# Query projection in unpadded 128-column tiles, laid into head slots through DRAM, with the VectorE exponential pairs placed anew

## The chip, the cores and the metric

The kernel runs on one core of a Trainium2 chip. The metric is device microseconds of one execution. Before the change the median of three runs is 865.13 us (864.38 to 865.44).

TensorE (PE) multiplies, ScalarE (ACT) evaluates exponentials, VectorE (DVE) and GpSimd (POOL) do elementwise work, and SyncE (SP) issues nearly all DMAs. Each engine works through its own list in order. Only semaphores tie the lists together.

## The reference

Two branches share the input x = A_q (2048 tokens by 640 features, bf16) and are mixed by a gate per token:

```python
g = _sigmoid((x * gate_w).sum(-1, keepdims=True))
a = _A_ref(x, A_k, A_v, A_shift_k, A_ssm_k, A_ssm_D)   # q * (long convolution of shifted k * v)
b = _B_ref(x, B_wq, B_wk, B_wv, B_wo)
return g * a + (1 - g) * b
```

Branch b is attention with 32 query heads of 20 features and one shared key and value head:

```python
q = (x @ wq).reshape(B, S, H, Dh)      # H = 32, Dh = 20, so wq is 640 x 640
k = x @ wk                             # 2048 x 20
v = x @ wv
scores = einsum("bhqd,bkd->bhqk", q, k) * (Dh ** -0.5)
o = einsum("bhqk,bkd->bhqd", softmax(scores), v)
return o.reshape(B, S, H * Dh) @ wo
```

Attention needs 32 x 2048 x 2048 exponentials. Branch a is a causal convolution along the tokens for each feature, done as a discrete Fourier transform by matrix products.

## The kernel before

**Attention tiles.** The 2048 queries are taken in four blocks I of 512. Within a block the 32 heads form 8 groups of 4. A group number G = 8 I + g runs from 0 to 31. For each group and each of 16 key chunks j, four 32-row matmuls (`score`, L1243) make four score tiles of 128 keys by 512 queries, one for each head slot r. So there are 32 x 16 x 4 = 2048 tiles. A head slot is 32 partitions: rows 32 r to 32 r + 19 of `qT` hold the 20 features of head 4 g + r, row 32 r + 20 holds an estimate of that query's norm (it makes a shift that keeps the exponential in range), and row 32 r + 21 holds a constant. `qT0` serves even blocks and `qT1` odd ones.

**Who does the exponential.** `stream` (L1197) strings the tiles together and cuts what is ACT's into units of three and two tiles by turns. L1280 is ACT's exponential of one unit, out of PSUM into `ETA` (three tiles) or `ETB` (two). The table `DVE_J` (L666) names, for each group, the key chunks of which two of the four tiles go to DVE instead. Such a pair costs DVE two PSUM reads (L1313, `dW`) and three passes over 128 x 1024 (L1325 and L1326, `dX`; L1328, `ETd`). `DVE_J` holds 108 pairs: 22, 31, 24 and 31 in the four blocks. L1333 multiplies the exponentials with the values into PSUM bank 6. At a group's end L1407 copies that bank to `acc`; then `norm` goes by four small DMAs on SP and one POOL product (L1419).

**The query projection.** `qproj` (L1140) works on padded weights: `wq_pad` has 1024 columns, 32 for each head, of which 20 are filled. POOL clears it (five memsets, L1032) and copies the weights in from `wqst` (L1024, and four copies at L1036). A group then takes five matmuls 128 x 512 (L1148), one DVE move out of PSUM that adds the constant row (L1159; ACT's L1161 for the first), and one square (L1163). For each batch of groups, matmuls with an indicator matrix (L1171) sum the squares by head, DVE takes an approximate root by integer arithmetic (L1177, `cr`), and one DMA (`crow`) puts the norms into rows 20, 52, 84 and 116. Block 0 is done in batches of 1, 2, 2, 2 and 1 groups, later blocks in two batches of four (`qproj_next`, L1737). Its PSUM banks are 7 and 5, which it shares with DVE's score tiles and with the convolution.

**The order of the work.** `Scheduler` (L172) plays the whole program through at build time. It has a cost for every operation (`c_dve`, `c_pool`, `c_act` and literals in the calls), a latency between engines (`LATS` before attention starts, `LATM` and `LATX` after), and priorities. It places each operation when its engine is free and its inputs are there, and it knows a port that DVE and POOL share (`port=True`, L508 to L513). The order that comes out is fixed in each engine's list. The two main streams of attention (scores, exponentials) keep their own order; everything else is fitted between. Matmuls on zeros (L1772) are put where PE would be idle.

**The convolution** (`kshift`, `conv`, `spectra`, `mac`, `inverse`) and the output projection fill PE, DVE and POOL between attention's pieces. The last block's part of the output is made by `part` and `tail`.

Of the kernel before, what the change touches and what calls it, by code (L numbers as in the profile page):

```python
# [5 lines left out]
dt = mybir.dt  # L6
# [18 lines left out]
        ("pool", "pool"): 0.0}  # L25
# [146 lines left out]
class Scheduler:  # L172
# [148 lines left out]
    def lat_of(self, op, a, b):  # L321
        if self.main_started:
            return LATM.get((a, b), LATX)
        return 0.03 if op.kind == "d" else LATS.get((a, b), LAT)
# [341 lines left out]
DVE_J = ((), (2,), (4, 6, 10, 14), (2, 6, 13, 14), (1, 2, 4, 11), (7, 12, 14), (3, 10), (2, 9, 11, 12), (1, 4, 7, 10, 12, 14), (1, 9), (1, 4, 8, 10, 14), (2, 7, 12), (2, 7, 8, 13), (2, 5, 9, 13), (6, 10, 13), (1, 3, 11, 13), (), (2, 11, 14), (1, 2, 4, 9), (1, 7, 9, 13), (2, 4, 6, 10, 14), (1, 7, 10, 14), (), (2, 7, 11, 14), (5, 6, 12, 14), (3, 7, 9, 12), (3, 6, 9, 10, 12), (13,), (2, 5, 6, 14), (4, 5, 8), (1, 4, 6, 9, 11, 14), (1, 2, 4, 5))  # L666
# [35 lines left out]
class Kernel:  # L702
# [59 lines left out]
    def alloc(self):  # L762
# [23 lines left out]
        sb("wq_pad", [128, NDC, 1024], BF16)  # L786
# [21 lines left out]
        sb("IndG4", [128, 4, 16], BF16)  # L808
# [14 lines left out]
        sb("cr", [16, 512], BF16)  # L823
# [22 lines left out]
        over("wqst", "qT1", 0, [128, NDC, D], BF16)  # L846
# [12 lines left out]
        over("wog", "wq_pad", 0, [128, 8, D], BF16)  # L859
# [6 lines left out]
        self.ps_bf = self.ps[:, :].bitcast(BF16)  # L866
        self.scr_o = nc.dram_tensor("scr_o", [4, 1024, 512], BF16).ap()
# [3 lines left out]
    def loads(self):  # L871
# [3 lines left out]
        for b in range(NB):  # L875
# [4 lines left out]
            if b == 0:  # L880
                self.dma(T["wqst"][:, :, 0:80], wq[:, :, 0:80], writes=[("wqst", 0)], prio=-8.5, lat=5.0)
# [6 lines left out]
        self.dma(T["wqst"][:, :, 80:640], wq[:, :, 80:640], writes=[("wqst", 1)], nbytes=716800, prio=-4,  # L888
# [5 lines left out]
    def consts(self):  # L894
# [28 lines left out]
        for n in ("IndG2", "IndG4"):  # L923
            P(lambda e, n=n: e.memset(T[n][:, :, :], 0.0), (), [n], 0.2, prio=-9.7)
# [34 lines left out]
    def tables2(self):  # L959
# [7 lines left out]
        for gl in range(4):  # L967
            self.dve(lambda e, gl=gl: e.tensor_copy(T["IndG4"][:, gl, gl:16:4], T["acol"][:, :]), ["acol"], ["IndG4"],
                     0.15, **k)

# [19 lines left out]
        for name, parts in (("Tsin", (("Tsin", 1), ("Tcos", 1), ("Tsin", -1), ("Tcos", -1))),  # L990
                            ("Tcos", (("Tcos", 1), ("Tsin", -1), ("Tcos", -1), ("Tsin", 1)))):
            for r, (src, sg) in enumerate(parts):
                for c in range(H):
# [5 lines left out]
                    self.pool(fn, [(src, c)], [(name, H + c, r), (name, H + c)], c_pool(256), prio=15.0 + c,  # L999
# [13 lines left out]
    def weights(self):  # L1013
# [9 lines left out]
        src = T["wqst"][:, :, :].rearrange("p k (h c) -> p k h c", c=20)  # L1023
# [3 lines left out]
    def weights2(self):  # L1027
        T = self.T
        dst = T["wq_pad"][:, :, :].rearrange("p k (h c) -> p k h c", c=32)
        src = T["wqst"][:, :, :].rearrange("p k (h c) -> p k h c", c=20)  # L1030
        for k in range(NDC):
            self.pool(lambda e, k=k: e.memset(T["wq_pad"][:, k, 128:1024].bitcast(I32), 0), (), [("wq_pad", g) for g in range(1, 8)], 0.45,  # L1032
                      prio=-8.9, after=[self.g.writer["sq", 0]])
        self.wq_cp = []
        for lo, hi in ((4, 8), (8, 16), (16, 24), (24, 32)):
            self.wq_cp.append(self.pool(lambda e, lo=lo, hi=hi: e.tensor_copy(dst[:, :, lo:hi, 0:20], src[:, :, lo:hi, :]),  # L1036
                      [("wqst", 1)], [("wq_pad", g) for g in range(lo // 4, hi // 4)], 0.75 if hi - lo == 4 else 1.5, prio=-4 + 0.01 * lo, name="wq_cp",
                      after=self.crow0 + [self.g.writer["kT4", NB - 1, 0]]))
# [101 lines left out]
    def qproj(self, I, gs, prio, banks, ng):  # L1140

        T = self.T
        qt = T[f"qT{I % 2}"]
        par = I % 2
        for gl, gi in enumerate(gs):
            gr = self.group("qp", prio, banks=banks)
            for dc in range(NDC):
# [4 lines left out]
                if dc == 0:  # L1152

                    o.deps.update(self.crow0 or ())
                    if self.crow0:
                        o.deps.add(self.g.writer["mcol"])
                    o.deps.update(self.g.readers.get((f"qT{par}", gi), ()))
            self.evac(gr, "dve", None, ["qup"], [(f"qT{par}", gi)], 0.7,
# [6 lines left out]
                     [(f"qT{par}", gi)], [("sq", gl)], 0.336 if I else 0.43, prio=-1500.0 if I == 0 and gs[0] < 3 else prio - 500, port=True,  # L1165
# [4 lines left out]
        for gl in range(nq):  # L1170
# [10 lines left out]
                 writes=[(f"qT{par}", gi) for gi in gs], nbytes=4 * nq * 1024, prio=pr, name="crow", lat=1.7)  # L1181
        if I == 0 and gs[0] == 0:
            self.crow0 = [o]

# [33 lines left out]
    def attention(self):  # L1218
# [19 lines left out]

        def score(e, bk, G, j, r, t=0):
# [10 lines left out]
        def QK(n):  # L1250
            un = units[n]
            I = min(un[-1][0], LASTG) // 8
            if I not in started:
                started.add(I)
                self.qproj_next(I)
                if I == NB - 1:
                    self.g.fence(["oT3", "part"], ["xT"])
                    self.g.fence(["wog"], ["wq_pad"])
# [3 lines left out]
            for p, (t, k, (G, j, r)) in enumerate(parts):  # L1262
                bk = base[n % 2] + k
                c = 0.003
                if p == len(parts) - 1 or parts[p + 1][0] > t:
                    c = 0.216 / min(split(x[0]) for u, _, x in parts if u == t)
                o = op("pe", lambda e, bk=bk, G=G, j=j, r=r, t=t: score(e, bk, G, j, r, t),
                       [self.kkey(split(G) * j + t), qkey(G)], [("ps", bk)], c,
# [15 lines left out]
        def DEXP(G, j):  # L1284
# [12 lines left out]
            for h, r in enumerate(self.on_dve[G, j]):  # L1297
# [7 lines left out]
                        [self.kkey(m * j + t) for t in range(m)] + [qkey(G)], 0.04)  # L1305
# [97 lines left out]
    def norm(self, I, g):  # L1403
# [8 lines left out]
        self.dve(lambda e: e.reciprocal(T["rcp"][:, :], T["den"][:, :]), ["den"], ["rcp"], 0.3, prio=p, name="rcp")  # L1412
# [22 lines left out]
    def part(self):  # L1435

        T = self.T
        for ci in range(4):
            for half in range(2):
# [3 lines left out]
                for g in range(6):  # L1443
# [5 lines left out]
                    ALU.mult, ALU.add), ["omgf", ("A", i)], [("part", ci)], c_dve(HD))  # L1449
# [27 lines left out]
    def tail(self):  # L1477
# [11 lines left out]
        for ci in range(fin[0]):  # L1489
            i = 4 * (NB - 1) + ci  # L1490
            osb = T[f"outsb{ci}"]
            for half in range(2):
                n0 = HD * half
                gr = self.group("op2s", -800.0 + ci, banks=(7, 6, 5))
                for g in (6, 7):
# [4 lines left out]
                    ALU.mult, ALU.add), ["omgf", ("part", ci)], [("outsb", ci)], c_dve(HD))  # L1500
# [37 lines left out]
    def kshift(self):  # L1538
# [7 lines left out]
        for b in range(NB):  # L1546
# [10 lines left out]
            ["ident", "wtap"], ["kdiag"], c_ps(2560), prio=16, port=True, name="ksh", after=[self.g.writer["kT4", NB - 1, 0], self.wq_cp[1]])  # L1557
# [24 lines left out]
    def conv(self):  # L1582
        T = self.T
        t0, per = 120.0, 100.0
        for i in range(NSC):

            self.dve(lambda e, i=i: e.tensor_scalar(T["xn"][:, i, :], T["xn"][:, i, :], T["gf"][:, i:i + 1], None,
                                                    ALU.mult), ["gf"], [("xg", i), ("xn", i // 4)], 0.4,
# [9 lines left out]
    def spectra(self, c, fc, base):  # L1598
# [7 lines left out]
        for kind in ("X", "K"):  # L1606
# [26 lines left out]
            if kind == "X":  # L1633
# [11 lines left out]
                [("K", p)], c_dve(256))  # L1645
# [186 lines left out]
```

## Time and profile before

| what | value |
|---|---|
| median of three runs | 865.13 us |
| the profiled execution | 866.22 us |
| its span, first to last instruction | 864.4 us |
| granted TensorE clock, mean | 0.998 |
| first exponential of attention (L1280) starts | 20.46 us |
| last exponential of attention starts | 857.79 us |
| DMA moved | 30.69 MB in 49728 packets |

The profiled execution is 1.1 us above the median, and its span is 1.8 us shorter than its time. Differences are worked out inside the span and set against the median.

A row of a group of instructions reads: line, engine, operation, output<-input with shapes, count | busy us, mean ns of one | idle us of the engine just before them, and what ended it. ACT's and PE's instructions overlap in their pipelines, so for ACT the distance between the ends of successive instructions is the honest cost, not the mean duration. A row of the timeline reads: start us, length us, engine, line, operation, count, and in brackets the idle time before it with its releaser. A row of windows reads: stretch, its length, and for each engine the busy us and the count.

### The profile page before, as it was taken

The page shows a single profiled execution, that of the slowest core. Times are in us where ns is not written, and L with a number is a line of the kernel's source. Part 1 is how long each engine was busy: PE and PEld are TensorE (multiplying, and loading weights), DVE is VectorE, ACT ScalarE, POOL GpSimd, SP SyncE. Part 2 cuts the span into 40 slices and gives each one's busy share as a digit, 9 for nine tenths or more (in the row PEclk, how much of TensorE's full clock was granted, in tenths as well). Part 3 has the DMA queues.
Part 4 walks back from the last instruction along what each step waited for, and adds up shares of the span by engine and source line. Part 5 has one row for each costly group of instructions (what it writes and reads, how often), then busy time and mean ns, then how long its engine had stood idle before and what let it go on. Part 6 is the DMA issues. An engine that isn't in the chain of part 4 may idle for free.

```text
span 864.4 us, 18503 instructions
## 1 busy us (share of the span) xinstructions
PE 840.7 (97%) x7963; PEld 350.2 (41%) x7963; DVE 782.3 (90%) x987; ACT 845.7 (98%) x755; POOL 375.7 (43%) x315
## 2 busy tenths in 40 slices
PE   8999999999999999999999999999999999999998
PEld 5234433344334433434434334444443434433334
DVE  7689999998999899999898989898869999898896
ACT  6999999999999999999999999999999999999997
POOL 4584000458764243655434475335776665000010
PEclk9999999999999999999999999999999999999999
DMA  6900010000100000020000020200010000401111
GB/s 172 236 14 9 20 45 20 16 19 8 44 20 21 20 14 17 13 44 20 20 14 8 20 45 20 53 20 8 26 38 20 15 2 24 102 30 60 43 35 44
DMA packets 49728, 30.69 MB, mean 36 GB/s; under 512 B 32493, under 2 KB 45678, under 8 KB 49646
## 3 DMA queue, kind: packets, MB, share of 16 engines
q1 hardware_dynamic: 49070, 29.29, 12.5%
q8 instruction: 62, 1.02, 0.5%
q10 hardware_dynamic: 576, 0.22, 0.1%
q14 instruction: 20, 0.16, 0.1%
HBM read 17.85 MB, written 6.02 MB: 28 GB/s over the span
## 4 chain that ended last, share of the span: by engine, by line
ACT 45%; PE 27%; DVE 24%; issue 2%; POOL 1%; POOLq 0%; DVEq 0%
ACT ETA L1280 27%; ACT ETB L1280 18%; PE ps L1243 8%; DVE dX L1326 6%; DVE ETd L1328 5%; DVE dX L1325 4%; PE ps L1333 4%; PE ps L1622 4%; DVE dW L1313 4%; PE ps L1690 3%; PE ps L1772 2%; PE ps L1720 2%; DVE qT L1159 1%; DVE X L1635 1%; PE ps L1777 1%
## 5 line engine op out<-in xcount | busy, mean ns | idle before, releaser
L1280 ACT ACTIVATE ETA<-ps 128x1536 bf16<-128x1536 f32 (+1 forms) x367 | 566.6, 1544 | 6.0 <-PE ps L1243 5.3
L1280 ACT ACTIVATE ETB<-ps 128x1024 bf16<-128x1024 f32 x366 | 411.2, 1123 | 0.2 <-PE ps L1243 0.2
L1243 PE MATMUL ps<-qT,kT 32*128 32x512 bf16 (+2 forms) x2176 | 304.1, 372 | 10.4 <-ACT ETA L1280 2.8
L1655 POOL TENSOR_TENSOR Pp<-X,K 128x1024 f32<-128x1024 bf16 (+1 forms) x80 | 150.7, 1896 | 130.1 <-DVE K L1643 62.9
L1243 PEld LDWEIGHTS ps<-qT,kT 32*128 32x128 bf16 x2176 | 78.1, 91 | 234.3 <-ACT ETB L1280 102.4
L1313 DVE TENSOR_SCALAR dW<-ps 128x512 f32<-128x512 f32 x216 | 147.0, 681 | 26.2 <-PE ps L1243 25.7
L1328 DVE SCALAR_TENSOR_TENSOR ETd<-dX,dW 128x1024 int16<-128x1024 f32 x108 | 158.5, 1467 | 3.0 <-PE ps L1333 2.7
L1326 DVE SCALAR_TENSOR_TENSOR dX<-dX,dW 128x1024 f32<-128x1024 f32 x108 | 154.1, 1427 | 0.7
L1333 PE MATMUL ps<-ETA,vaug 128*32 128x512 bf16 (+2 forms) x1174 | 154.1, 372 | 0.1
L1325 DVE SCALAR_TENSOR_TENSOR dX<-dW 128x1024 f32<-128x1024 uint16 x108 | 151.5, 1403 | 1.3
L1333 PE MATMUL ps<-ETB,vaug 128*32 128x512 bf16 (+2 forms) x778 | 148.1, 373 | 0.2 <-ACT ETA L1280 0.2
L1655 POOL TENSOR_TENSOR AB<-Pp 128x256 bf16<-128x256 f32 x80 | 71.7, 896 | 72.7 <-DVE dX L1326 26.6
L1622 PE MATMUL ps<-ssm_kT,Tcs 128*128 128x256 bf16 x600 | 89.8, 274 | 2.5 <-DVE dW L1313 2.0
L1690 PE MATMUL ps<-AB,Tcs 128*128 128x256 bf16 x600 | 89.7, 276 | 0.3 <-DVE dW L1313 0.2
L1622 PE MATMUL ps<-kv,Tcs 128*128 128x256 bf16 x600 | 87.1, 275 | 0.7 <-DVE dW L1313 0.4
L1419 POOL TENSOR_TENSOR oTn<-acc,rbc 128x512 bf16<-128x512 f32 x24 | 38.8, 1616 | 85.6 <-DMA rbc<-scr_d 67.3
L1655 POOL TENSOR_TENSOR Pp<-Pp 128x512 f32<-128x512 f32 x40 | 53.7, 1342 | 42.3 <-DVE dX L1325 12.9
L1622 PEld LDWEIGHTS ps<-ssm_kT,Tcs 128*128 128x128 bf16 x600 | 50.6, 98 | 38.5 <-issue 26.8
L1690 PEld LDWEIGHTS ps<-AB,Tcs 128*128 128x128 bf16 x600 | 51.6, 98 | 34.2 <-issue 25.7
L1622 PEld LDWEIGHTS ps<-kv,Tcs 128*128 128x128 bf16 x600 | 49.8, 98 | 35.1 <-issue 24.0
L1772 PE MATMUL ps<-Tcs,zeros 128*32 128x512 bf16 (+1 forms) x724 | 61.5, 383 | 0.4 <-DVE acc L1407 0.3
L1419 POOL TENSOR_TENSOR oT<-acc,rbc 128x512 bf16<-128x512 f32 x7 | 10.1, 1449 | 108.3 <-DMA rbc<-scr_d 58.1
(136 smaller groups left out, 664.9 us busy)
## 6 DMA issues: line engine op xcount, KB each, us to landing
rbc<-scr_d SPq DMA_DIRECT2D x31, 256.0 KB
scr_o<-oTn SPq DMA_DIRECT2D x24, 128.0 KB, 1.7
kv<-in_A_v_dram SPq DMA_DIRECT2D x4, 640.0 KB, 5.0
out_dram<-outsb SPq DMA_DIRECT2D x15, 160.0 KB, 1.8
xn<-in_A_q_dram SPq DMA_DIRECT2D x3, 640.0 KB, 7.9
oTp<-scr_o SPq DMA_DIRECT2D x12, 160.0 KB, 2.5
wog<-in_B_wo_dram SPq DMA_DIRECT2D x4, 200.0 KB
wo<-in_B_wo_dram SPq DMA_DIRECT2D x4, 200.0 KB
```

The lines of the kernel that those rows point to most:

```text
L1243: return e.matmul(self.bank(bk, n, n * t), T["kT4"][32 * r:32 * r + 32, 128 * jt:128 * jt + 128], T[k][32 * r:32 * r + 32, g, q0:q0 + n], ...
L1280: op("act", lambda e: e.activation(et(n)[:, 0:w], self.ps[:, lo:lo + w], ACT.Exp, scale=SCALE), [("ps", base[n % 2] + k) for k in range(le ...
L1313: self.evac(gr, "dve", lambda e, bk, c=c: e.tensor_scalar(W[:, c], self.bank(bk), SCALE * LOG2E * 128.0, 128.0 * (127 - KDN) - 32768.0, AL ...
L1325: V(lambda e: e.scalar_tensor_tensor(X[:, :], w, DP, w, ALU.add, ALU.mult), [kW], ["dX"], c_dve(1024), **k)
L1326: V(lambda e: e.scalar_tensor_tensor(X[:, :], X[:, :], DQ, w, ALU.add, ALU.mult), [kW], ["dX"], c_dve(1024), **k)
L1328: V(lambda e: e.scalar_tensor_tensor(E, X[:, :], DA, W[:, :], ALU.mult, ALU.add), [kW, "dX"], [("ETd", pe)], c_dve(1024), **k)
L1333: return op("pe", lambda e: e.matmul(self.bank(b, n)[32 * r:32 * r + 32, :], T[va][:, j, :], src, start=(j == 0), stop=(j == NSC - 1), til ...
L1419: self.pool(lambda e: e.tensor_tensor(out, T["acc"][:, :], T["rbc"][:, :], ALU.mult), ["acc", "rbc"], [key], 1.27, prio=p, port=True, name ...
L1622: self.mm(gr, lambda e, bk, lhs=lhs, rhs=rhs, comp=comp, n=n: e.matmul(self.bank(bk, 256, 256 * comp), lhs, rhs, start=(n == 0), stop=(n = ...
L1655: f = lambda e: e.tensor_tensor(out, a, b, alu)
L1690: self.mm(gr, lambda e, bk, lhs=lhs, fc=fc, comp=comp, h=h: e.matmul(self.bank(bk, 256, 256 * h), lhs, AB[:, fc, :, comp, :], start=(fc == ...
L1772: sch.filler, *sch.filler2 = ([[lambda e, r=r, st=st, b=b, n=n: e.matmul(self.bank(b, n)[32 * r:32 * r + 32, :], self.T["zeros"][:, 0:32], ...
```

## The change

The projection drops the padding for all but the first two groups of block 0. A tile is now 128 consecutive columns of the raw `wq`, five tiles for 640 columns, so that a tile holds 6.4 heads that cross the head slots. `qtiles` moves each tile from PSUM to a staging area (in `qT1` for block 0, in the used-up part of `xT` for later blocks), squares it, and stores it to a DRAM tensor `scr_q`. Four DMAs, one for each slot r, then read it back with the 20 features of a head as 20 partitions. One product with a new indicator `IndT` (made by `heads`) gives the norms of all heads of the block at once, and four DMAs put them in place. The constant row and the zero padding no longer come with the projection: `qfixed` writes them beforehand, for `qT0` by one POOL copy and one DMA that repeats it, for `qT1` by eight POOL copies. Groups 0 and 1 of block 0 keep the old way, with `wq_pad` cut to 256 columns, and block 0 starts its tiles at tile 1. A score matmul waits on three records now (features, norms, slot).

Apart from that, costs and latencies in the planner are changed at some ten places, and `DVE_J` is written anew: 110 pairs, with 21, 32, 27 and 30 in the four blocks.

```diff
-        ("pool", "pool"): 0.0}
+        ("pool", "pool"): 0.075}
...
-            return LATM.get((a, b), LATX)
+            return 0.19 if op.name == "dqk" else LATM.get((a, b), LATX)
...
-DVE_J = ((), (2,), (4, 6, 10, 14), (2, 6, 13, 14), (1, 2, 4, 11), (7, 12, 14), (3, 10), (2, 9, 11, 12), (1, 4, 7, 10, 12, 14), (1, 9), (1, 4, 8, 10, 14), (2, 7, 12), (2, 7, 8, 13), (2, 5, 9, 13), (6, 10, 13), (1, 3, 11, 13), (), (2, 11, 14), (1, 2, 4, 9), (1, 7, 9, 13), (2, 4, 6, 10, 14), (1, 7, 10, 14), (), (2, 7, 11, 14), (5, 6, 12, 14), (3, 7, 9, 12), (3, 6, 9, 10, 12), (13,), (2, 5, 6, 14), (4, 5, 8), (1, 4, 6, 9, 11, 14), (1, 2, 4, 5))
+DVE_J = ((), (3,), (4, 6, 11, 14), (3, 8, 14), (1, 2, 5, 10), (7, 12, 13), (3, 11), (2, 9, 10, 12), (1, 4, 7, 11, 12, 14), (1, 12), (2, 4, 8, 10, 14), (2, 7, 11), (1, 6, 9, 13), (5, 8, 13, 14), (6, 8, 13), (1, 3, 10, 13, 14), (12,), (2, 9, 14), (2, 8, 9, 13), (1, 8, 9, 13), (2, 4, 6, 11, 12, 14), (1, 8, 11, 12), (), (1, 8, 11, 13, 14), (2, 6, 10, 13, 14), (7, 14), (1, 3, 6, 9, 12), (6, 11, 14), (4, 7, 12), (1, 7, 10), (1, 4, 6, 8, 10, 12, 14), (3, 5))
...
     def weights2(self):
-        for k in range(NDC):
-            self.pool(lambda e, k=k: e.memset(T["wq_pad"][:, k, 128:1024].bitcast(I32), 0), ...
-        self.wq_cp = []
-        for lo, hi in ((4, 8), (8, 16), (16, 24), (24, 32)):
-            self.wq_cp.append(self.pool(lambda e, lo=lo, hi=hi: e.tensor_copy(dst[:, :, lo:hi, 0:20], src[:, :, lo:hi, :]), ...
+        self.pool(lambda e: e.memset(T["wq_pad"][:, :, 128:256].bitcast(I32), 0), (), [("wq_pad", 1)], 0.5, prio=-8.9,
+                  after=[self.g.writer["sq", 0]])
+        self.wq_cp = self.pool(lambda e: e.tensor_copy(dst[:, :, 4:8, 0:20], src[:, :, 4:8, :]), [("wqst", 1)],
+                               [("wq_pad", 1)], 0.75, prio=-4, name="wq_cp", ...
+    def qfixed(self, I):
+        qt, lo = T[f"qT{I}"], 0 if I else 2
+        f = lambda e, a, b: e.tensor_copy(qt[:, a:b, :], T["qup"][:, 0:1].unsqueeze(2).to_broadcast([128, b - a, 512]))
+        if I:
+            for g in range(8):
+                self.pool(lambda e, g=g: f(e, g, g + 1), ["qup"], [(f"qT{I}", g, x) for x in range(5)], c_pool(512),
+                          prio=40.0 + g, name="qfix", after=self.crow0)
+            return
+        self.pool(lambda e: f(e, 2, 3), ["qup"], [("qT0", 2, x) for x in range(5)], c_pool(512), prio=-5.0,
+                  name="qfix", after=self.crow0)
+        self.dma(qt[:, 3:8, :], qt[:, 2:3, :].to_broadcast([128, 5, 512]), reads=[("qT0", 2, 0)],
+                 writes=[("qT0", g, x) for g in range(3, 8) for x in range(5)], nbytes=655360, prio=0.0, name="qfix")
...
+    def heads(self):
+        self.pool(lambda e: e.iota(u.rearrange("p (t r g) -> p t r g", t=NDC, r=4), [[128, NDC], [-20, 4], [-80, 8]], ...
+        self.dve(lambda e: e.tensor_scalar(v, u, 0.0, None, ALU.is_ge), ["acc"], ["accv"], 0.25, **k)
+        self.dve(lambda e: e.scalar_tensor_tensor(T["IndT"][:, :, :].rearrange("p t c -> p (t c)"), u, 20.0, v, ALU.is_lt, ...
...
+    def qtiles(self, I, t0, prio, banks):
+        for t in range(t0, NDC):
+            gr = self.group("qp", prio, banks=banks)
+            for dc in range(NDC):
+                o = self.mm(gr, lambda e, bk, t=t, dc=dc: e.matmul(
+                    self.bank(bk), T["wq"][:, dc, 128 * t:128 * t + 128], T["xT"][:, dc, 512 * I:512 * I + 512], ...
+            x = self.evac(gr, "dve", None, (), [("qs", I, t)], 0.7,
+                          alts={"dve": ((lambda e, bk, o=stage[t]: e.tensor_copy(o, self.bank(bk))), ...
+            self.dve(lambda e, t=t: e.tensor_tensor(T[f"sq{t}"][:, :], stage[t], stage[t], ALU.mult), [("qs", I, t)],
+                     [("sq", t)], 0.336, prio=prio - 500, port=True, name="sq")
+            self.dma(self.scr_q[I][128 * t:128 * t + 128, :], stage[t], reads=[("qs", I, t)], writes=[("scr_q", I, t)],
+                     nbytes=131072, prio=prio - 500, name="q_st")
+        gr = self.group("q2", prio - 500, banks=banks)
+        for t in range(t0, NDC):
+            self.mm(gr, lambda e, bk, t=t: e.matmul(self.bank(bk)[0:32, :], T["IndT"][:, t, :], T[f"sq{t}"][:, :], ...
...
+        for r in range(4):
+            self.dma(qt[32 * r:32 * r + 20, g0:8, :], src[r][:, g0:8, :], reads=[("scr_q", I, t) for t in range(t0, NDC)],
+                     writes=[(par, g, r) for g in range(g0, 8)], nbytes=163840, prio=prio - 500, name="q_ld", lat=2.6)
+        for r in range(4):
+            self.dma(qt[32 * r + 20:32 * r + 21, g0:8, :], cr[8 * r + g0:8 * r + 8, :], reads=["cr"], ... name="crow", lat=1.7)
...
+        def qks(G, r):
+            n, g = qkey(G)
+            return [(n, g, r), (n, g, 4), (n, g, 5 + r)]
...
     def qproj_next(self, I):
         if I < NB:
-            for b in range(2):
-                self.qproj(I, list(range(4 * b, 4 * b + 4)), 150.0 * (I - 1) + 60 + 60 * b, (7, 5), 4)
+            self.qtiles(I, 0, 150.0 * (I - 1) + 60, (7, 5))
...
-        for b, gs in enumerate(([0], [1, 2], [3, 4], [5, 6], [7])):
-            self.qproj(0, gs, 0.61 if b == 0 else 3.0 + 6 * b, ALLB if b == 0 else (7, 5), 2)
+        self.qproj(0, [0], 0.61, ALLB, 2)
+        self.weights2()
+        self.qproj(0, [1], 9.0, (7, 5), 2)
...
+        self.heads()
+        self.qfixed(0)
+        self.qtiles(0, 1, 12.0, (7, 5))
+        self.qfixed(1)
```

The other planner costs that change are those of the table copies (+0.15), the reciprocal (0.3 to 0.16), the scaled input rows (0.4 to 0.3), the output moves (+0.06), one spectrum move (+0.03), and one POOL product, `mac`'s first, set to 2.125.

## The prediction

> **What bounds the kernel now.** I read the page's shares first, then the chain, then ACT's timeline.
>
> ```profile
> PE 840.7 (97%) x7963; PEld 350.2 (41%) x7963; DVE 782.3 (90%) x987; ACT 845.7 (98%) x755; POOL 375.7 (43%) x315
> ACT 45%; PE 27%; DVE 24%; issue 2%; POOL 1%; POOLq 0%; DVEq 0%
> ```
>
> ACT is busy for 98% of the span and has the largest share of the chain. PE's 97% is not a full load: 724 of its matmuls are products of zeros that the planner puts where PE would be idle. So ACT sets the pace, and the question is what it costs ACT to get through its list. ACT's timeline answers that:
>
> ```profile
> 20.46 1.45 ACT L1280 ACTIVATE ETA<-ps 128x1536 bf16<-128x1536 f32 x1 [0.17 <-PE ps L1243]
> 21.81 1.02 ACT L1280 ACTIVATE ETB<-ps 128x1024 bf16<-128x1024 f32 x1
> 22.71 1.46 ACT L1280 ACTIVATE ETA<-ps 128x1536 bf16<-128x1536 f32 x1
> ...
> 857.79 1.16 ACT L1280 ACTIVATE ETA<-ps 128x1024 bf16<-128x1024 f32 x1
> ```
>
> The first ends at 21.91, the third at 24.17: a unit of three and a unit of two, five tiles, take 2.26 us, or 0.452 us a tile. ACT has 2048 - 2 x 108 = 1832 tiles, so 1832 x 0.452 = 828.1 us without a pause. From 20.46 to 858.95 are 838.5 us, so **10.4 us are stalls**. Before it lie 20.5 us of start, after it 5.5 us of tail. Span = 20.5 + 828.1 + 10.4 + 5.5 = 864.4.
>
> Where do the stalls sit? In stretches of 27 us (columns: PE, PEld, DVE, ACT, POOL busy with counts, clock, DMA):
>
> ```profile
> 108.00:135.00 27.00, 26.03 (x235) 8.49 (x232) 26.85 (x38) 26.59 (x25) 1.57 (x1) 1.00 0.16 36
> 135.00:162.00 27.00, 25.79 (x230) 9.69 (x228) 27.00 (x38) 26.49 (x24) 5.82 (x4) 1.00 0.05 18
> ...
> 648.00:675.00 27.00, 25.41 (x235) 11.14 (x233) 26.79 (x29) 26.18 (x24) 16.59 (x14) 1.00 0.05 16
> ```
>
> ACT loses half a microsecond and more where DVE is full (26.8 to 27.0 of 27). DVE doesn't stand on the path itself; it makes PE wait, and PE is in order. One such place, in the projection:
>
> ```profile
> 119.09 0.74 DVE L1159 TENSOR_SCALAR qT<-ps,cols 128x512 bf16<-128x512 f32 x1
> 119.88 0.39 PE L1148 MATMUL ps<-xT,wq_pad 128*128 128x512 bf16 x1 [0.77 <-DVE qT L1159]
> 120.69 1.45 ACT L1280 ACTIVATE ETA<-ps 128x1536 bf16<-128x1536 f32 x1 [0.41 <-PE ps L1243]
> ```
>
> A projection matmul waits 0.77 us for its bank, the score matmuls queue behind it, and ACT stands for 0.41 us.
>
> **The change, part by part.** *Pairs.* 110 instead of 108 takes 4 tiles from ACT: 4 x 0.452 = **-1.8 us**, the one term that is certain to be on the path. On DVE a pair costs two moves and three passes (sums over 108 pairs; the mean follows the busy time):
>
> ```profile
> L1328 DVE SCALAR_TENSOR_TENSOR ETd<-dX,dW 128x1024 int16<-128x1024 f32 x108 | 158.5, 1467 | 3.0 <-PE ps L1333 2.7
> L1326 DVE SCALAR_TENSOR_TENSOR dX<-dX,dW 128x1024 f32<-128x1024 f32 x108 | 154.1, 1427 | 0.7
> L1325 DVE SCALAR_TENSOR_TENSOR dX<-dW 128x1024 f32<-128x1024 uint16 x108 | 151.5, 1403 | 1.3
> L1313 DVE TENSOR_SCALAR dW<-ps 128x512 f32<-128x512 f32 x216 | 147.0, 681 | 26.2 <-PE ps L1243 25.7
> ```
>
> That is 1.47 + 1.43 + 1.40 + 2 x 0.68 = 5.66 us, so two pairs add 11.3 us of DVE.
>
> *DVE's part of the projection.* Three rows carry it:
>
> ```profile
> L1159 DVE TENSOR_SCALAR qT<-ps,cols 128x512 bf16<-128x512 f32 x31 | 22.8, 739 | 7.1 <-PE ps L1148 7.1
> L1163 DVE TENSOR_TENSOR sq<-qT 128x512 bf16<-128x512 bf16 x32 | 15.2, 489 | 1.5 <-ACT qT L1161 1.4
> L1177 DVE TENSOR_SCALAR cr<-ps 16x512 int16<-16x512 int32 (+1 forms) x11 | 7.4, 672 | 1.4 <-PE ps L1171 1.4
> ```
>
> After it there are 1 + 4 + 15 = 20 moves, 19 of them plain copies. The trace has no bf16 copy of 512 out of PSUM; the f32 copy of 512 (L1407, median 681 ns) and L1313 (681 ns) are the nearest, so 0.68 us each and 13.7 in all, -9.1. Squares go from 32 to 21 (11 x 0.49 = -5.4), roots from 11 to 6 (5 x 0.67 = -3.4), the four casts of the old indicator go (-0.7), two small operations come (+0.4). Sum -18.2, and with the pairs **DVE -6.9 us**: 775 of 864. Each later block saves 4.7 of it (eight moves, eight squares and two roots are 11.2 us; five, five and one are 6.5). With the pairs the load moves by block: block 0 -5.7 for one pair less, block 1 +5.7 - 4.7, block 2 +17.0 - 4.7 = +12.3, block 3 -5.7. (Block 3's queries are made during block 2.) That costs nothing on the path as long as DVE's idle time covers it; between 432 and 648 DVE is busy 189 of 216 us, so 27 us cover 12.
>
> *PE.* 160 projection matmuls become 10 + 20 + 75 = 105. Five in a row take 1.24 us with the last's 0.38, so 0.215 each: -11.8 us. Products for the norms go from 32 to 21: -2.4. This lies under ACT and buys nothing directly; zeros take its place. Where it counts is the bank: three eighths fewer moves that a matmul can wait for.
>
> *POOL.* Four of the five clears (L1032, 0.47 us each) and three of the four weight copies (3.0 - 0.5 = 2.5 us) go; one index fill (about 0.25, by the fill of 128 at 0.24) and nine broadcast copies of 128 x 512 come. The nearest row is `vneg` (L1221, 128 x 512 bf16, 664 ns); a strided copy of half the size (L996) has a median of 769 ns, so twice that, 1.5, is the upper end, and 0.5 the lower. I take 0.66: 6.0 us, of which 5.3 for `qT1`. POOL has 15 us idle after 76 and 25 more before 117, and nobody waits for `qT1` before group 8, at 235 us. The POOL time costs nothing.
>
> But there is a rule that speaks against it. The Trainium skill, "SBUF — State Buffer", section "SBUF: two separate sides", has the port pair that VectorE shares with GpSimd as an exclusive lock, against which a VectorE operation with two SBUF inputs is fully blocked while a GpSimd operation reads. All three passes of a pair are of that kind. The trace agrees: a pass that has the port to itself takes 1.16 to 1.22 us, and
>
> ```profile
> 141.19 1.27 POOL L1419 TENSOR_TENSOR oTn<-acc,rbc 128x512 bf16<-128x512 f32 x1 [22.05 <-DMA rbc<-scr_d]
> 141.25 2.30 DVE L1326 SCALAR_TENSOR_TENSOR dX<-dX,dW 128x1024 f32<-128x1024 f32 x1
> ```
>
> this one takes 1.08 longer. By the rule eight copies block DVE for 8 x 0.66 = 5.3 us, between 75 and 115, where DVE is full. By the rows it is less: passes average 0.2 us above 1.22, POOL being started near their ends (1.43 against 1.22 over 324 passes makes 68 us, for 315 POOL operations, 0.22 each), so 8 x 0.22 = 1.8. I take 1.8 of DVE; even 5.3 is covered by block 0's -5.7. Cover gone, it would be at most 5.3 on the path.
>
> *The start.* The index fill and the first broadcast copy want POOL at about 17 us, when the first norm DMA lands, while DVE makes the last small operands before the first exponential at 20.46. Lower end 0, upper end one copy, 1.2; beside POOL's casts of 18.73 to 19.11 DVE's small operations take no longer than without (0.15 to 0.29), so I take **+0.2**.
>
> *DMAs.* 19 stores of 128 KB, 16 loads of 160 KB (120 in block 0), one spread of 640 KB and 18 instead of 11 norm rows go on SP. Issue by the rows of like kind: 19 x 0.33 + 16 x 0.55 + 0.6 + 7 x 0.55 = 19.6 us of SP over the run, at most 8 x 0.55 = 4.4 in one stretch. Queued behind are `norm`'s four DMAs: in group 2 they go from 80.84 (`den`) to 92.11 (the store), 11 us of a group's 26, so 4.4 more is hidden. Landing is 1.7 us for the like stores of `scr_o`, 2.5 for the like loads of `oTp`. The waits that matter are those of the score matmuls. In block 0, six moves were done at 45.2; now it is group 1 and four tiles, five moves, so the last store lands near 47.5, four loads are issued by 50, landed by 52.5 (by 60 at the 7.9 us that loads took in the crowded start), norms by 56 to 63. Group 2's scores begin after group 1's last, near 77: at least 14 us to spare. Later blocks load more than 100 us ahead, once the old group 7 is read. POOL clears nothing for it; the spread comes first, at 18 to 20, and pushes the key and value loads by 0.6 us of SP and some 2 of transfer; they feed the convolution, which starts at 147. All hidden: **0**.
>
> *Order.* The two stalls at 120.69 and 144.97 (0.41 and 0.22, the second behind L1171) are the projection's own. Three eighths fewer groups, and one sum for two: **-0.4**. What the new costs and the new places do to the remaining 9.8 us no row shows. Ends: -5 (half of it goes) and +7 (below). DVE and PE are both lighter, so I take a small gain, **-0.8**.
>
> **Sum.** -1.8 + 0.2 - 0.4 - 0.8 = **-2.8 us**: span 861.6, and off the median 865.13 - 2.8 = **862.3 us**. The tail's code is the same, and groups 28 to 31 hold 15 pairs instead of 17, so DVE comes to it no later: 0, within 0.5.
>
> **Rivals.** *The tiles are paid back* (865.0): ACT has 1.8 less to do, but 0.45 us for each tile comes back as stalls where DVE is full. For it: block 1 keeps DVE at 95% (205 of 216 us between 216 and 432). Against: the total load falls. -1.8 + 1.5 + 0.2 = -0.1.
>
> *Slower, by an overfull block 2* (870.5): three more pairs in groups 16 to 23. The worst stretch of the trace is 648 to 729, where DVE is at 26.8, 26.9 and 24.2 of 27 and ACT's unit ends slip by 3.4 us in 81, 4.2%. At that rate 216 us would lose 9.1 instead of the 1.9 they lose now: -1.8 + 7.2 = +5.4. It decides once the extra stalls pass 1.8 + 1.7 = 3.5. Against: after the change this block has still 15 us of DVE idle.
>
> *A better order* (858.1): half of the stalls go, -1.8 - 5.2. For it: each stall is a place where the plan and the chip disagree, and costs were moved towards the rows (the reciprocal is 0.24 here, planned at 0.3; the output moves 0.54, planned at 0.40). Against: many stalls sit where DVE is full, not misjudged.
>
> **Chances.** Between two builds 0.2% (1.7 us) is about what this measurement can tell from none. Likeliest (862.3, own range 860.8 to 863.8) 0.62; paid back 0.20; better order 0.12; slower 0.06. Below 863.4: 0.58 of the likeliest, the better order, 0.05 of the paid-back: 0.75. Above 866.9: 0.06 and 0.01. Between: 0.18. The range for 8 in 10 runs from 859.3 to 865.4: it takes in the likeliest, most of the paid-back case and part of the better order.
>
> **What would show it.** ACT's units end 2.26 us apart still, 731 of them instead of 733, and first to last about 835.4 us. L1148's matmuls with raw weights 95, DVE near 775 us busy. No ACT idle near 77 us with scores behind a load: if there is, the block-0 chain is wrong. POOL's copies of 128 x 512 between 65 and 115, with DVE passes of 1.9 and more beside them only if the lock bites. The first exponential later than 20.7 would put the start wrong; stalls above 12 us with DVE full in block 2 would be the slow rival, and stalls under 7 the better order.

## The result, and the profile after

The median falls from 865.32 to **862.43 us** (861.01 to 863.49, eight runs each), a ratio of 0.9966 [0.9954, 0.9977]. The forecast was 862.3. The profiled execution takes 861.71 us with a span of 859.9, 4.5 less than before's; of these 4.5, 1.6 are the two executions' own place about their medians (0.9 above, 0.7 below).

The page's shares and chain:

```profile
PE 836.1 (97%) x8073; PEld 349.3 (41%) x8073; DVE 788.3 (92%) x968; ACT 841.7 (98%) x753; POOL 378.1 (44%) x317
ACT 78%; PE 17%; DVE 4%; DMA 0%; issue 0%; POOL 0%; POOLq 0%
```

ACT's share of the chain goes from 45% to 78%, DVE's from 24% to 4%: there are fewer places left where something other than ACT decides. DVE was not relieved as a whole, though: 788.3 us against 782.3.

ACT's timeline:

```profile
20.63 1.45 ACT L1347 ACTIVATE ETA<-ps 128x1536 bf16<-128x1536 f32 x1 [0.17 <-PE ps L1310]
...
852.98 1.45 ACT L1347 ACTIVATE ETA<-ps 128x1536 bf16<-128x1536 f32 x1
```

From 20.63 to 854.43 are 833.8 us. ACT has 2048 - 220 = 1828 tiles, at 0.452 us 826.3, so **7.5 us are stalls**; the start is 20.6 and the tail 5.5. Against before that is +0.2 (start), -1.8 (tiles), -2.9 (stalls) and 0 (tail), together -4.5. At the medians the change is -2.9, so the stalls' part is about -1.3 there if the other terms hold; the numbers below are those of the two profiled executions. To see where the stalls sit, take each unit's end minus the end before it minus its own 1.34 us (three tiles) or 0.92 us (two):

| ACT's stalls, us | before | after |
|---|---|---|
| 27 to 54 us | 0.0 | 3.4 |
| everywhere else | 10.4 | 4.1 |

So the -2.9 is made of two larger numbers: **-6.3 over the whole run, and +3.4 at one place that before does not have**. The stretches that stood in the prediction for the first number (columns: PE, PEld, DVE, ACT, POOL busy with counts, clock, DMA share, GB/s):

```profile
27.00:54.00 27.00, 24.85 (x208) 8.82 (x209) 17.59 (x26) 23.89 (x22) 17.76 (x21) 0.94 0.76 187
108.00:135.00 27.00, 26.32 (x224) 9.07 (x222) 26.96 (x45) 27.00 (x25) 2.26 (x2) 1.00 0.28 70
135.00:162.00 27.00, 26.77 (x254) 11.01 (x253) 26.95 (x34) 27.00 (x25) 14.18 (x12) 1.00 0.05 16
648.00:675.00 27.00, 26.35 (x249) 10.23 (x246) 25.34 (x26) 27.00 (x25) 18.25 (x12) 1.00 0.05 17
```

From 108 to 162 DVE is as full as it was, 26.95 us of 27, and yet ACT loses nothing. Only the first row is bad: ACT at 23.89 and a granted clock of 0.94.

**The place at 46 us.** PE and ACT, out of the timeline:

```profile
43.47 0.38 PE L1310 MATMUL ps<-qT,kT 32*128 32x512 bf16 x1 [1.93 <-DMA qT<-cr]
45.14 1.45 ACT L1347 ACTIVATE ETA<-ps 128x1536 bf16<-128x1536 f32 x1 [1.80 <-PE ps L1310]
...
46.38 1.89 PE L1632 MATMUL ps<-kdiag,kTr 128*128 128x128 bf16 x16
...
48.84 1.45 ACT L1347 ACTIVATE ETA<-ps 128x1536 bf16<-128x1536 f32 x1 [1.31 <-PE ps L1310]
```

A lone score matmul, for DVE's first pair of group 1, waits 1.93 us for the norms of group 1 (`qT<-cr`). Behind it in PE's list stand ACT's next scores, so ACT stands for 1.80 us. The second stall, 1.31 us, waits for scores behind the sixteen small matmuls of L1632 (a step of the convolution). The clock says why they are slow:

```profile
41.00:43.50 2.50, 0.57 (x4) 0.13 (x3) 0.00 (x0) 2.34 (x3) 0.00 (x0) 1.00 1.05 372
43.50:46.00 2.50, 2.50 (x24) 0.59 (x24) 1.71 (x3) 0.86 (x1) 1.33 (x2) 0.83 0.07 23
46.00:48.00 2.00, 2.00 (x19) 1.63 (x16) 1.43 (x2) 1.53 (x2) 1.43 (x3) 0.50 0.26 73
```

PE is busy for 0.57 us of the 2.5; after that gap the granted clock falls to 0.83 and 0.50. One late DMA is paid for twice, once by the wait and once by the clock. The Trainium skill, "TensorE: Matmul & The Clock Gate", section "Why this matters for your kernels", asks that PE have no idle gaps above some 3 us, because after them the clock goes to half. By that figure a wait of 1.93 us would have been free of the second cost; this trace shows the half clock after it, so the measurement decides.

Why is the DMA late? DVE had made the norms at 36.47. DVE's line, and SP's own timeline:

```profile
35.79 0.68 DVE L1198 TENSOR_SCALAR cr<-ps 8x512 int16<-8x512 int32 x1 [1.33 <-PE ps L1192]
...
34.05 4.20 SPq L1615 DMA_TRANSPOSE kTr<-in_A_k_dram  x1
38.30 0.58 SPq L725 DMA_DIRECT2D kv<-in_A_v_dram  x1
38.93 0.50 SPq L725 DMA_DIRECT2D scr_q<-qT  x1
39.48 0.60 SPq L725 DMA_DIRECT2D qT<-cr  x1
```

The 4 KB of `qT<-cr` are issued at 39.48, behind a transposing key load that holds SP for 4.20 us, 640 KB of values and a store of 128 KB; they have landed at 43.47, when PE goes on. The planner had the issue at 37.31 and the landing at 41.08, because it takes 3.3 us for each key load. Before sends its norm row behind the same loads, at 40.69, later still, but there DVE's first read of a group-1 tile comes later too, and nobody is waiting:

```profile
46.12 0.69 DVE L1313 TENSOR_SCALAR dW<-ps 128x512 f32<-128x512 f32 x1 [0.44 <-PE ps L1243]
```

### The profile page after: what moved, and what is told of

It is laid out like the page before. It is cut to its first block, busy times and chain, and to the rows that moved or that the text cites. A ratio compares the mean times of both kernels' runs of the same rounds, so it can differ in the third digit from the quotient of the medians.

```text
span 859.9 us, 18774 instructions
## 1 busy us (share of the span) xinstructions
PE 836.1 (97%) x8073; PEld 349.3 (41%) x8073; DVE 788.3 (92%) x968; ACT 841.7 (98%) x753; POOL 378.1 (44%) x317
## 4 chain that ended last, share of the span: by engine, by line
ACT 78%; PE 17%; DVE 4%; DMA 0%; issue 0%; POOL 0%; POOLq 0%
ACT ETA L1347 47%; ACT ETB L1347 32%; PE ps L1310 5%; PE ps L1689 3%; PE ps L1400 3%; PE ps L1757 2%; PE ps L1843 1%; PE ps L1848 1%; DVE dW L1380 1%; DVE dX L1392 1%; PE ps L1511 1%; PE ps L1217 1%; DVE dX L1393 1%; PE ps L1075 0%; DMA qT<-cr 0%; DVE ETd L1395 0%
## 5 line engine op out<-in xcount | busy, mean ns | idle before, releaser
L1347 ACT ACTIVATE ETA<-ps 128x1536 bf16<-128x1536 f32 x366 | 579.6, 1584 | 5.6 <-PE ps L1310 5.4
L1347 ACT ACTIVATE ETB<-ps 128x1024 bf16<-128x1024 f32 x365 | 424.5, 1163 | 0.0
L1722 POOL TENSOR_TENSOR Pp<-X,K 128x1024 f32<-128x1024 bf16 (+1 forms) x80 | 145.3, 1824 | 140.6 <-DVE K L1710 42.3
L1392 DVE SCALAR_TENSOR_TENSOR dX<-dW 128x1024 f32<-128x1024 uint16 x110 | 165.5, 1505 | 1.6
L1395 DVE SCALAR_TENSOR_TENSOR ETd<-dX,dW 128x1024 int16<-128x1024 f32 x110 | 163.5, 1486 | 0.3
L1393 DVE SCALAR_TENSOR_TENSOR dX<-dX,dW 128x1024 f32<-128x1024 f32 x110 | 159.8, 1452 | 0.8
L1722 POOL TENSOR_TENSOR AB<-Pp 128x256 bf16<-128x256 f32 x80 | 67.7, 846 | 83.6 <-DVE dX L1393 32.0
L1722 POOL TENSOR_TENSOR Pp<-Pp 128x512 f32<-128x512 f32 x40 | 57.0, 1425 | 51.2 <-DVE dX L1393 20.3
L1843 PE MATMUL ps<-Tcs,zeros 128*32 128x512 bf16 (+1 forms) x900 | 74.0, 383 | 1.0 <-DVE acc L1474 0.9
L1689 PEld LDWEIGHTS ps<-ssm_kT,Tcs 128*128 128x128 bf16 x600 | 50.7, 98 | 38.7 <-issue 28.1
L1486 POOL TENSOR_TENSOR oTn<-acc,rbc 128x512 bf16<-128x512 f32 x24 | 42.9, 1787 | 36.4 <-DVE ETd L1395 21.5
```

What stands on the lines that cost most here:

```text
L1347: op("act", lambda e: e.activation(et(n)[:, 0:w], self.ps[:, lo:lo + w], ACT.Exp, scale=SCALE), [("ps", base[n % 2] + k) for k in range(le ...
L1392: V(lambda e: e.scalar_tensor_tensor(X[:, :], w, DP, w, ALU.add, ALU.mult), [kW], ["dX"], c_dve(1024), **k)
L1393: V(lambda e: e.scalar_tensor_tensor(X[:, :], X[:, :], DQ, w, ALU.add, ALU.mult), [kW], ["dX"], c_dve(1024), **k)
L1395: V(lambda e: e.scalar_tensor_tensor(E, X[:, :], DA, W[:, :], ALU.mult, ALU.add), [kW, "dX"], [("ETd", pe)], c_dve(1024), **k)
L1486: self.pool(lambda e: e.tensor_tensor(out, T["acc"][:, :], T["rbc"][:, :], ALU.mult), ["acc", "rbc"], [key], 1.27, prio=p, port=True, name ...
L1689: self.mm(gr, lambda e, bk, lhs=lhs, rhs=rhs, comp=comp, n=n: e.matmul(self.bank(bk, 256, 256 * comp), lhs, rhs, start=(n == 0), stop=(n = ...
```

## The experiments

Two questions were left: whether the norm DMA's place is the whole of the +3.4, and what made the -6.3, the lighter projection or the planner's costs.

**The changed kernel a second time**, unedited, to see whether the place at 46 us belongs to the kernel.

> The changed kernel once more, as the yardstick for the three beside it. Expected: about 862.4 us, and in its timeline again a score matmul of group 1 that waits some 2 us for the norm rows near 43 us, then a granted clock of 0.5 for about 2 us, and two ACT stalls of 1.8 and 1.3 us near 45 and 49. If these stalls are an accident of one execution, they are absent or far smaller here.

Measured: 862.62 us (861.59 to 863.48), 0.9967 [0.9956, 0.9979]. In its profiled execution ACT's stalls are 9.6 us, 5.5 of them between 46 and 52 and 4.1 elsewhere. The wait for the norms is there, 2.8 us long, and so is the clock (windows as above):

```profile
43.85 0.60 PE L1310 MATMUL ps<-qT,kT 32*128 32x512 bf16 x1 [2.82 <-DMA qT<-cr]
...
43.50:46.00 2.50, 2.15 (x13) 0.44 (x13) 1.47 (x3) 0.00 (x0) 0.73 (x2) 0.57 0.05 9
46.00:48.00 2.00, 2.00 (x15) 0.29 (x13) 0.24 (x1) 1.39 (x1) 2.00 (x4) 0.50 0.19 66
48.00:50.50 2.50, 2.50 (x23) 1.81 (x21) 2.34 (x3) 1.10 (x3) 0.08 (x1) 0.50 0.46 131
```

The place is the kernel's own; its price differs between executions (3.4 and 5.5 us), while the rest is steady at 4.1. The dearer one has the longer wait (2.82 us against 1.93) and is at half clock from 43.8 to 50.7 us instead of 45.1 to 48.5.

**The norm row ahead of the value load.** Only the planner's issue time for the transposing key load is changed; it then puts the norm row, and with it two stores, ahead of the value load in SP's list. The lists of PE, DVE, ACT and POOL stay as they are.

```diff
-            x.iss = 3.3
+            x.iss = 4.5
```

> The changed kernel with one planner number altered: the issue time of the key loads (transposing DMAs) is planned at 4.5 us instead of 3.3. The orders on PE, DVE, ACT and POOL stay word for word the same; on SP alone the norm rows of group 1 (and two stores) move ahead of the last value load of 640 KB. Theory A (the late norm rows make both early stalls, the second through the halved clock): the norm rows land 2 us or more earlier, the 3.3 us of stalls near 45 and 49 vanish, the clock stays at 1.00 there, and the time is about 859.1 us, 3.3 below the changed kernel. Rival (PE would stand at that place anyway, for the exponentials or for a bank): stalls of 2 us or more stay, time above 861.5.

Measured: **858.95 us** (857.79 to 859.2), 0.9922 [0.9909, 0.9936]: 3.5 below the changed kernel, 3.7 below its second measurement. SP's timeline, the sixteen matmuls and the windows of this kernel:

```profile
34.05 4.51 SPq L1615 DMA_TRANSPOSE kTr<-in_A_k_dram  x1
38.60 0.59 SPq L725 DMA_DIRECT2D qT<-cr  x1
39.23 0.92 SPq L725 DMA_DIRECT2D scr_q<-qT  x2
40.19 0.46 SPq L725 DMA_DIRECT2D kv<-in_A_v_dram  x1
...
43.64 1.07 PE L1632 MATMUL ps<-kdiag,kTr 128*128 128x128 bf16 x16
```

```profile
41.00:43.50 2.50, 2.50 (x27) 0.69 (x26) 1.71 (x3) 2.50 (x4) 1.16 (x2) 1.00 0.63 152
43.50:46.00 2.50, 2.50 (x30) 1.30 (x28) 2.16 (x3) 2.50 (x3) 1.61 (x3) 1.00 0.67 231
46.00:48.00 2.00, 1.80 (x19) 0.41 (x16) 2.00 (x3) 2.00 (x3) 1.37 (x1) 1.00 0.02 6
```

The row is issued only 0.9 us earlier, but ahead of the 640 KB and the store instead of behind them. ACT is full in all three windows, the clock stays at 1.00, and the sixteen matmuls of L1632 take 1.07 us instead of 1.89. No stall is left between 27 and 54 us; in the whole run there are 4.6. The +3.4 is shown: it is this DMA's place in SP's list.

Right behind that stretch a smaller stall of the same kind appears. It is the first score of group 2, for DVE's first pair, and it waits for the norms that came over the new way:

```profile
53.23 0.37 PE L1310 MATMUL ps<-qT,kT 32*128 32x512 bf16 x1 [0.49 <-DMA qT<-cr]
...
54.91 1.45 ACT L1347 ACTIVATE ETA<-ps 128x1536 bf16<-128x1536 f32 x1 [0.35 <-PE ps L1310]
```

ACT reaches group 2 only some 24 us later: DVE's pairs are scored that far ahead. In the changed kernel the same matmul comes at 56.00 and does not wait.

**DVE's saved time given back.** On top of the last kernel, two reductions of 128 x 512 ahead of each square of the projection from block 1 on, planned at nothing: 30 x 0.67 = 20.1 us of useless DVE work.

```diff
+  e.tensor_reduce(T["junk"][:, c:c+1], stage[t], AX.X, ALU.max)      # two of these
   e.tensor_tensor(T[f"sq{t}"][:, :], stage[t], stage[t], ALU.mult)
```

> As the one before, with the same orders, and 30 useless reductions of 128x512 on DVE, two ahead of each square of blocks 1 to 3, at about 0.6 us each: some 18 us, as much DVE time as the new projection saves in all. Theory B (the other stalls fell from 7 to 4 us and more because DVE is lighter): they come back, 4 to 8 us more than the one before, so about 864 to 867. Rival (the stalls fell because the new order and the new places fit the chip better, and DVE has room to spare): 0 to 2 us more, so 859 to 861.

Measured: 882.26 us (880.96 to 882.52), 1.0191 [1.0177, 1.0205]: **+23.3 us** over norm_first, 1.16 for each us added (1.23 if the ends in which they overlap are not counted) and far more than either theory expected. A group, a window and a chain of waits (line numbers are one higher here than in the changed kernel):

```profile
L1228 DVE TENSOR_REDUCE junk<-xT 128x1 f32<-128x512 bf16 x30 | 19.0, 671 | 0.0
```

```profile
108.00:135.00 27.00, 23.30 (x156) 7.37 (x155) 25.85 (x44) 20.04 (x19) 1.26 (x1) 0.81 0.22 61
```

```profile
120.37 1.70 PE L1690 MATMUL ps<-kv,Tcs 128*128 128x256 bf16 x8 [1.59 <-DVE dW L1381]
...
122.93 1.45 ACT L1348 ACTIVATE ETA<-ps 128x1536 bf16<-128x1536 f32 x1 [2.33 <-PE ps L1311]
```

The stalls are where the projections are (7.6 us between 108 and 162, 7.2 between 216 and 270, 8.8 between 432 and 486). A convolution matmul waits for a bank that a late DVE read still holds, ACT's scores wait behind it, and the clock drops again, to 0.81 on the mean of the stretch. In norm_first DVE is busy for 26.3 to 27.0 us of every 27 in these stretches (22.5 from 243 to 270), so there is hardly any idle time in them, and that of other stretches is no help, since every engine keeps its list. Here DVE time that the plan doesn't know was paid in full, and a little more. This says what unplanned DVE time costs in these stretches; it does not say what the change's planned saving of 18 us was worth, since there the plan moved with it.

**The old projection with the new pairs and costs.**

```diff
-        ("pool", "pool"): 0.0}
+        ("pool", "pool"): 0.075}
...
-            return LATM.get((a, b), LATX)
+            return 0.19 if op.name == "dqk" else LATM.get((a, b), LATX)
...
-["den"], ["rcp"], 0.3, prio=p, name="rcp")
+["den"], ["rcp"], 0.16, prio=p, name="rcp")
...
```

(The other costs of the change likewise, and `DVE_J` as in the changed kernel.)

> The kernel before (padded projection by groups) with the new pair table (110 pairs) and the new planner costs: the change without its projection. If the two moved pairs pay by themselves, 863.5 or less, as 4 tiles are 1.8 us of ACT. If they fit only the lighter projection (theory C), DVE is overfull where the old projection runs, mostly in groups 16 to 23 and at the end, and the time is 868 to 878.

Measured: 884.94 us (883.32 to 885.07), 1.0219 [1.0204, 1.0235]; ACT's stalls are 23.7 us. The plan itself has 16.1 of these, at the same places (the largest at 575.3 in the plan, 4.4 us; at 577.4 on the chip, 4.25), and ends at 875.8, against 854.1 for the changed kernel: nearly all of the loss was planned. This table of pairs was not made for this projection, so the run shows only that the 110 pairs as placed need the lighter one. What a projection is worth with pairs made for it needs other runs.

**Two by two: projection and planner costs, each with its own table.** Four kernels: before's projection or the changed one (with the norm row first), before's costs or the changed ones. For each a table of pairs was searched by the planner's own end time, 108 pairs for the old projection and 110 for the new. The edits, in the order old_old (on before), old_new (on before, all the changed costs), new_old (on norm_first, all of before's costs), new_new (on norm_first); each comes with its own table, of which the first groups are shown where it is the whole edit:

```diff
-DVE_J = ((), (2,), (4, 6, 10, 14), (2, 6, 13, 14), ...
+DVE_J = ((), (10,), (3, 12), (5, 8, 12, 13, 14), ...
```

```diff
-        ("pool", "pool"): 0.0}
+        ("pool", "pool"): 0.075}
...
```

```diff
-        ("pool", "pool"): 0.075}
+        ("pool", "pool"): 0.0}
...
```

```diff
-DVE_J = ((), (3,), (4, 6, 11, 14), (3, 8, 14), ...
+DVE_J = ((), (1, 8, 9, 14), (5,), (13,), ...
```

> Old projection, old planner costs, 108 pairs in a table found anew with the planner (its plan ends at 856.5, that of the kernel before at 855.8). One corner of four: each has a table that the planner fits to it, so that projection and costs can be told apart without a table that fits neither. If tables of like plans do alike on the chip, 864 to 867. If what the plan doesn't see is left to the table's luck, it may lie 3 us and more away from the kernel before.

> Old projection, new planner costs, 108 pairs in a table found for them (plan 856.8). Theory E (the other stalls fell because costs nearer to the chip's leave fewer surprises): 860 to 862, half of the unplanned stalls gone. Theory F (they fell because the projection is lighter): no better than the corner with both old, 864 to 868.

> New projection with the norm rows of group 1 moved ahead, old planner costs, 110 pairs in a table found for them (plan 853.9). Theory E: unplanned stalls stay near 10, so 863 to 866. Theory F: 858 to 861, no worse than the corner with both new.

> New projection with the norm rows of group 1 moved ahead, new planner costs, 110 pairs in another table (plan 854.0, that of the run with the norm rows moved 854.1). If a plan's end tells the chip's time, about 859 as that run; how far it is off is the measure for table luck, against which the other three corners have to be read.

| median, us | before's costs | changed costs | difference |
|---|---|---|---|
| old projection, 108 pairs | 871.07 (868.85 to 871.37) | 865.76 (862.89 to 868.96) | -5.3 |
| new projection, 110 pairs | 865.68 (864.04 to 867.59) | 860.98 (860.39 to 861.48) | -4.7 |
| difference | -5.4 | -4.8 | |

In these four, costs and projection differ by like amounts, and they add: -5.3 or -4.7 for the costs, -5.4 or -4.8 for the projection with its two pairs. No theory gets its forecasts throughout: new_old lies where theory E had it (863 to 866), old_new where theory F had it, yet well below old_old, which is itself 4 us above its own range. ACT's stalls less the plan's own are 14.7 and 9.4 us in the first row, 11.2 and 6.1 in the second. So in each row the plan made with the changed costs is nearer to what the chip does.

But the table alone moves as much. old_old has before's costs, projection and number of pairs, plans an end 0.7 us later (856.5 against 855.8), and runs 6.1 us slower than before, measured beside it (865.01). new_new plans 0.1 us earlier than the changed kernel (854.0 against 854.1) and runs 2.0 slower than norm_first. What the planner calls equal is spread over several us on the chip, so how the change's own -6.3 divides between lighter projection, costs and a lucky table stays open. Each corner is a single table, so even that the first two count is made likely by the like differences in both rows and both columns, and not shown.

**More pairs.** Since norm_first leaves ACT with 4.6 us of stalls, its only other large term is the tiles: 112 and 113 pairs on norm_first, with tables searched in the same way.

```diff
-DVE_J = ((), (3,), (4, 6, 11, 14), (3, 8, 14), ...
+DVE_J = ((), (2,), (4, 7, 11, 14), (1, 3, 10, 14), ...
```

```diff
-DVE_J = ((), (3,), (4, 6, 11, 14), (3, 8, 14), ...
+DVE_J = ((), (2,), (4, 6, 11, 14), (3, 6, 14), ...
```

> The changed kernel with the norm rows of group 1 moved ahead and two pairs more, 112, in a table found for them (plan 852.1 against 854.1 with 110). If the planner's end carries over to the chip within the 2 us that another table of the same plan costs, 857 to 859; if DVE has no room for two pairs more (5.8 us each, 11.6), the stalls take back the 1.8 us that ACT saves, and more: 860 to 864.

> The same with 113 pairs (plan 851.9, with 1.0 us of stalls in the plan itself). By the plan 857 to 859; if the room on DVE ends here, worse than with 112 by 1 us or more.

Measured: 860.29 us (858.34 to 860.86), 0.9937 [0.9925, 0.995], and 857.8 us (857.75 to 860.92), 0.9916 [0.9902, 0.9929]. Two pairs more are worth 1.8 us of ACT, but 112 comes out 1.3 slower than norm_first, its stalls being 7.4 instead of 4.6. With 113 three of five runs are near 857.8; the profiled one, at 860.92, has stalls of 3.4 and 0.4 us at 307.7 and 310.4, and 9.1 in all. norm_first and pairs_113 can't be told apart, and both are faster than the changed kernel. The tiles go to DVE for little: the spread between tables is as large as what a pair brings.

## Why the prediction was right, and why partly by luck

The total was right to 0.1 us. Term by term:

- **Pairs, -1.8: right.** Units still end 2.26 us apart, 731 of them; first to last 833.8 us where 835.4 was expected.
- **Start, +0.2: not contradicted.** 20.63 against 20.46. Two other executions of this code start at 20.13 and 20.56, so 0.2 can't be told from nothing.
- **Tail, 0: right**, 5.5 us.
- **"All hidden: 0" for the DMAs: this is the step that failed.** Its chain takes ACT's scores near 77 us as the first user of the new rows. The first user is DVE, whose pairs are scored ahead of ACT's: group 2's first score is at 56.00 in the changed kernel, and at 53.23, behind a wait of 0.49 us, in norm_first. So the 14 us to spare were not there, though in the changed kernel it cost nothing. What did cost was group 1, which the step leaves out. It keeps the old way, and its norm row goes through the same SP queue; the plan, with DVE's first pair of group 1 placed earlier, made PE need the row at 41.54, where its wait begins (before's DVE reads its first tile of group 1 at 46.12). The measured cost is +3.4 us (3.5 by norm_first). The prediction did count SP's issues behind which things are queued, yet only for `norm`'s four DMAs from group 2 on, not for 34 to 44 us.
- **"Order", -0.4 - 0.8 = -1.2: right in sign, far too small.** Stalls outside the place above fell by 6.3 (5.4 if all of the 0.9 that before's profiled execution lies above its median belongs here). The rival with a better order had -5.2 for this term and 0.12 of the chance; it was the better account of it. The reason given against it, that stalls sit where DVE is full and not misjudged, is wrong: at 108 to 162 DVE is as full as before and ACT no longer waits. That it matters instead whether DVE is where the plan has it fits dve_back, but was not tested by itself.
- **The two errors cancel, and that is luck**: -1.2 + 0 was predicted; -6.3 + 3.4 = -2.9 came in the profiled executions, about -1.3 at the medians. Without the failed step the time would have been norm_first's 858.95, below the range.
- **The rivals.** The tiles are not paid back in the full stretches. Block 2 did not overfill: between 432 and 648 ACT's stalls are 1.6 us (before: 1.9), most of them at 500.3 and 503.6.

DVE's sum was half right. (Its list by block leaves out what block 0 saves, on its own projection and on block 1's, so its entries add up to +1.9 and not to -6.9.) Its part of the projection fell from 46.1 to 27.6 us, -18.5 where -18.2 stood; the copies and squares are these, out of the groups of after:

```profile
L1224 DVE CAST xT<-ps 128x512 bf16<-128x512 f32 x15 | 10.1, 674 | 0.0
L1227 DVE TENSOR_TENSOR sq<-xT 128x512 bf16<-128x512 bf16 x15 | 6.1, 424 | 0.0
...
L1392 DVE SCALAR_TENSOR_TENSOR dX<-dW 128x1024 f32<-128x1024 uint16 x110 | 165.5, 1505 | 1.6
L1395 DVE SCALAR_TENSOR_TENSOR ETd<-dX,dW 128x1024 int16<-128x1024 f32 x110 | 163.5, 1486 | 0.3
L1393 DVE SCALAR_TENSOR_TENSOR dX<-dX,dW 128x1024 f32<-128x1024 f32 x110 | 159.8, 1452 | 0.8
```

A copy took 0.674 us (0.68 was taken). The pairs, however, are 638.5 us for 110, 5.80 each against 5.66, so they add 27.4 us and not 11.3: of their 330 passes 183 lie beside a POOL operation, where it was 168 of 324, and such a pass takes 1.70 us on average (before: 1.64), one by itself 1.21. That is why DVE reads 788.3 and not 775, and the time did not follow it.

POOL's eight broadcast copies between 77 and 92 us were the place of the rule about the port. A copy by itself takes 0.61 us (0.66 was taken). Four of them met a pass: in two cases the pass waited (1.51 and 1.60 us against 1.21), in the other two the copy did (1.62 and 1.68 us against 0.62), with the pass at 1.21 and 1.16. That is 0.7 us of DVE, where the rows gave 1.8; the 5.3 let DVE wait for all eight.

## What to carry to other kernels

When results are re-routed through a queue, look for the first user of everything on that queue, and not for the user of the largest transfer: 4 KB behind 640 KB cost 3.5 us here, because DVE's pairs are scored ahead of ACT's tiles, and one number in the plan took them back. In an order fixed at build time, what an engine's load is worth depends on whether the plan knows it: unplanned DVE time was paid at about 1.2 us per us where DVE was nearly full already. And plans with the same end differed by 2 to 6 us on the chip, so a gain of that size from a new table is no proof of the idea behind it. A total that comes out right is no proof of its terms; check each against the stretch that it speaks of.

## What the runs showed of the hardware that was not expected

The clock falls after shorter gaps than the 3 us above. It is no matter of this DMA: at the end of a group, where the planner puts no zeros into PE's list until DVE has copied bank 6 to `acc`, the changed kernel shows it too (PE's lines, windows, and an exponential behind them):

```profile
497.01 0.39 PE L1310 MATMUL ps<-qT,kT 32*128 32x512 bf16 x3 [0.95 <-ACT ETA L1347]
497.93 0.39 PE L1310 MATMUL ps<-qT,kT 32*128 32x512 bf16 x2 [0.53 <-ACT ETB L1347]
...
496.00:498.00 2.00, 0.52 (x8) 0.18 (x5) 2.00 (x3) 2.00 (x3) 0.86 (x2) 1.00 0.00 0
498.00:500.00 2.00, 2.00 (x16) 0.80 (x16) 1.97 (x4) 2.00 (x2) 0.44 (x1) 0.78 0.04 4
500.00:502.00 2.00, 2.00 (x15) 0.52 (x13) 2.00 (x3) 1.79 (x3) 0.88 (x1) 0.50 0.00 0
...
503.64 1.45 ACT L1347 ACTIVATE ETA<-ps 128x1536 bf16<-128x1536 f32 x1 [0.82 <-PE ps L1310]
```

PE idles for 1.5 us of two, in two pieces. The clock is at 0.50 from 499.1 to 502.5, beginning 1.2 us after the last piece's end (at the place of the norm row from 45.1 to 48.5, 1.7 us after it; 3.4 us both times). ACT stands for 0.18 and 0.82 us (at 500.31 and 503.64). Before has the same near 707 to 710, with 0.91 and 0.42, although its idle pieces there are only 0.17, 0.53 and 0.20 us. In neither kernel did ACT stop during the gap itself; it stopped during the slow matmuls after it.

The twelve traces together have 18 such stretches between the start and the tail. Ahead of 17 of them PE's idle pieces within 3.4 us add up to 1.48 us or more, in one piece or several; the exception is before's, just named. The largest such sum that no half clock follows is 1.37 us. The half clock sets in at the end of the gap or up to some 2 us after it; in the second profile of the changed kernel it does so at the end and lasts 6.8 us.
